# Windowed attention with a mixture of adapters: instruction order from a list scheduler, contiguous score columns, and q and k on 128 partitions

## The chip, the cores and the metric

The kernel runs on one core of one Trainium2 chip. The metric is the device time of one execution in microseconds (us). Executions of one kernel differ by one or two per cent, and the clock that TensorE is granted differs between them too (1.00 is full speed). "Slow" here means over 1.5% above the fastest run of the same kernel in the same group of runs. A profile gives the span from the first to the last instruction; the time of a run is some 1.8 to 2.1 us longer than its span.

Engine names: PE is TensorE's matmuls and PEld its weight loads, DVE is VectorE, ACT is ScalarE, POOL is GpSimd, SP is SyncE, whose queue issues most of the DMA transfers. L396 is line 396 of the kernel that is profiled, so line numbers change from kernel to kernel.

## The reference

```python
# q, k, v: (B=8, H=8, S=576, D=64) float32
scores = (1/sqrt(D)) * q @ k.T
mask   = abs(i - j) <= 32                      # sliding window
attn   = softmax(where(mask, scores, -1e9))
x      = (attn @ v) as (B*S=4608, H*D=512)
# mixture of adapters: E=8 experts of rank r=16, the best two per row
logits = x @ w_gate                            # (4608, 8)
w      = softmax over the two largest logits
out    = x + sum over the two of  w_e * (x @ A[e]) @ B[e]
```

## The kernel before

The work falls into 32 units, one for each pair of heads of each batch (8 batches of 4 units). For a unit, TensorE transposes q and k (`tp`), and the results are copied to SBUF (`qT` and half of `kT` by VectorE, the other half of `kT` by ScalarE). Then come score tiles (`ps`: two mask matmuls and eight score matmuls each), exp on ScalarE (`PT`), the product with v (`po`, "PV" below) and the normalisation on VectorE (`rc`, a RECIPROCAL, then `xb`). After four units the batch's adapters follow: transposes `tx`, logits and low-rank products `pz`, a chain of about ten small VectorE operations (the gate), `zs`, its transpose `tz`, the product `pd`, a ScalarE copy `obt` and the stores. PSUM, the memory that TensorE writes its results to, holds three tiles of 1024 float32 columns (`ps`, `po`, `pz` and `pd` share them; "two-bank tiles" is the prediction's name for them) and two of 1024 float16 columns (the transposes).

The parts that the change and the argument touch (cuts are marked):

```python
ob_pool = tc.alloc_tile_pool(name="ob", bufs=3)
pw = tc.alloc_tile_pool(name="pw", bufs=3, space=bass.MemoryType.PSUM)
pt = tc.alloc_tile_pool(name="pt", bufs=2, space=bass.MemoryType.PSUM)
# ... q and k as loaded and as cast by GpSimd: 96 partitions x 3 groups
raw[b, w] = load_pool.tile([96, 3, 2, NP, 2 * D], F32, ...)
qk[b, w] = cast_pool.tile([96, 3, 2, NP, 2, D], F16, ...)
# ... scores: the two rows of a pair are interleaved in the output columns
        nc.tensor.matmul(
            out=ps[:, i].rearrange("p (k j) -> p j k", j=2),   # stride 2
            lhsT=kTs[u % NQ][:, a, :],
            rhs=qTs[u % NQ][:, :, 32 * a:32 * a + 64], ...)
# ... gate, second part: small VectorE operations on SBUF tensors
    nc.vector.tensor_tensor(out=is2, in0=is2, in1=bcast(dm, 2, E), op=ALU.mult)
    nc.vector.tensor_tensor(out=gate, in0=is1, in1=is2, op=ALU.add)
    nc.vector.tensor_tensor(out=gate, in0=gate, in1=bcast(s, 2, E), op=ALU.mult)
# ... the fixed program order, one unit per turn
for u in range(NU):
    # loads of batch b+2 on nc.sync, casts of batch b+1 on nc.gpsimd
    transposes(u + 2, 0); transposes(u + 2, 1)
    # score(...) for the tiles of unit u+1
    # a piece of the adapters of batch b-1 (moe_out / moe_zl / moe_zT)
    pv(u)
    # another piece of them (moe_xT / moe_gate / moe_out)
```

The softmax here doesn't subtract the row's maximum and nothing guards it: scores larger than these inputs give would overflow.

Of the kernel before, what the change touches and what calls it, by code (L numbers as in the profile page):

```python
# [9 lines left out]
F16 = mybir.dt.float16  # L10
# [14 lines left out]



@with_exitstack
def kernel(
# [18 lines left out]
    NB = 9  # L48
# [25 lines left out]
    def raw_tiles(b):  # L74
        for w in range(2):
            raw[b, w] = load_pool.tile([96, 3, 2, NP, 2 * D], F32, tag=f"r{w}",
                                       name=f"r{w}")
            qk[b, w] = cast_pool.tile([96, 3, 2, NP, 2, D], F16, tag=f"c{w}",
                                      name=f"c{w}")
        raw[b, 2] = load_pool.tile([128, NP * NB, D], F32, tag="r2", name="r2")  # L80

    def load_qk(b, w, eng, n0=0, n1=NP):
        src = (q, k)[w][b]
        if n1 - n0 == NP:
            src = src.rearrange("h (g p j) d -> g p h (j d)", g=3, j=2)
            for g in range(3):
                eng.dma_start(out=raw[b, w][:, g].rearrange("p e n c -> p (e n) c"),
                              in_=src[g])
        else:
            src = src.rearrange("(e n) (g p j) d -> e g p n (j d)", e=2, g=3, j=2)  # L90
            for g in range(3):
                for e in range(2):
                    eng.dma_start(out=raw[b, w][:, g, e, n0:n1], in_=src[e, g][:, n0:n1])

    def load_v(b, eng, n0=0, n1=NP):
        src = v[b].rearrange("(e n) (a p j) d -> e j p (n a) d", e=2, p=32, j=2)
        for e in range(2):
            for j in range(2):
                p0 = 64 * e + 32 * j
                eng.dma_start(out=raw[b, 2][p0:p0 + 32, NB * n0:NB * n1],  # L100
                              in_=src[e, j][:, NB * n0:NB * n1])

    def cast_qk(b, w, eng, n0=0, n1=NP):
        for g in range(3):
            eng.tensor_copy(  # L105
                out=qk[b, w][:, g, :, n0:n1].rearrange("p j n e d -> p e n j d"),
                in_=raw[b, w][:, g, :, n0:n1].rearrange("p e n (j d) -> p e n j d", j=2))

# [13 lines left out]
    raw_tiles(0)  # L122
    for n0 in (0, 2):
        load_qk(0, 0, nc.sync, n0, n0 + 2)
        load_qk(0, 1, nc.scalar, n0, n0 + 2)
        load_v(0, nc.sync, n0, n0 + 2)

    ident = const.tile([128, 128], F16)
    make_identity(nc, ident)


    mask = const.tile([128, 4, 128], F16)
    nc.gpsimd.memset(mask, 0.0)
    for i in range(4):
        jk = i % 2
        blk = mask[32 * i:32 * i + 32]
        nc.gpsimd.affine_select(out=blk, in_=blk, compare_op=ALU.is_ge, fill=NEG,
                                base=-jk, channel_multiplier=-2,
                                pattern=[[0, 4], [1, 128]])
        nc.gpsimd.affine_select(out=blk, in_=blk, compare_op=ALU.is_ge, fill=NEG,  # L140
                                base=64 + jk, channel_multiplier=2,
                                pattern=[[0, 4], [-1, 128]])
# [10 lines left out]

    init_qkT(0)
    init_qkT(1)
    nc.vector.memset(PTs[0], 0.0)
    init_vbd(0)
    nc.vector.memset(PTs[1], 0.0)
# [17 lines left out]
    def transposes(u, which):  # L176
        b, n = divmod(u, NP)
        src = qk[b, which].rearrange("p g j n e d -> p g j n (e d)")
        tp = pt.tile([128, 1024], F16, tag="t", name="tp")
        for g in range(3):  # L180
            for j in range(2):
                if which == 0:
                    o = tp[:, 288 * j + 96 * g:288 * j + 96 * g + 96]
                else:
                    o = tp[:, 192 * g:192 * g + 192].rearrange(
                        "p (a j k) -> p a j k", a=3, j=2)[:, :, j]
                nc.tensor.matmul(  # L187
                    out=o, lhsT=src[:, g, j, n],
                    rhs=ident[0:96, 0:96], is_transpose=True, start=True, stop=True)
        if which == 0:  # L190
            nc.vector.tensor_copy(
                out=qTs[u % NQ][:, :, 16:304],
                in_=tp[:, 0:S].rearrange("p (j s) -> p j s", j=2))
        else:
            kt = tp[:, 0:S].rearrange("p (a k) -> p a k", k=64)
            nc.vector.tensor_copy(out=kTs[u % NQ][0:64, :, 0:64], in_=kt[0:64])  # L196
            nc.scalar.copy(out=kTs[u % NQ][64:128, :, 64:128], in_=kt[64:128])  # L197

    def score(t):
        ps = pw.tile([128, TB, 128], F32, tag="w", name="ps")  # L200
        for i in range(0, TB, 4):
            nc.tensor.matmul(out=ps[:, i:i + 4], lhsT=ident, rhs=mask,  # L202
                             start=True, stop=False)
        for i in range(TB):
            u, a = divmod(TB * t + i, NB)
            nc.tensor.matmul(  # L206
                out=ps[:, i].rearrange("p (k j) -> p j k", j=2),
                lhsT=kTs[u % NQ][:, a, :],
                rhs=qTs[u % NQ][:, :, 32 * a:32 * a + 64],
                start=False, stop=(i % 4 == 3))  # L210
        nc.scalar.activation(out=PTs[t % NPT][:, :, 64:192], in_=ps,  # L211
                             func=AF.Exp, scale=1.0 / float(D) ** 0.5)

    xs = {}

    def pv(u):
        b, n = divmod(u, NP)
        if n == 0:
            xs[b] = x_pool.tile([128, NG, DD], F16, tag="x", name="xb")
        po = pw.tile([128, 1024], F32, tag="w", name="po")  # L220
        for g in range(NG):
# [9 lines left out]
        pog = po[:, 0:GS * NG].rearrange("p (g c) -> p g c", c=GS)[:, :, 0:2 * VD]  # L231
# [6 lines left out]


    st = {}  # L240

    def moe_xT(b, g):
        if g == 0:
            st[b, "xT"] = moe_pool.tile([128, NG, 4, 128], F16, tag="xT", name="xT")
        tp = pt.tile([128, 1024], F16, tag="t", name="tx")
        for c in range(4):
            nc.tensor.matmul(out=tp[:, 128 * c:128 * c + 128],  # L247
                             lhsT=xs[b][:, g, 128 * c:128 * c + 128],
                             rhs=ident, is_transpose=True, start=True, stop=True)
        nc.vector.tensor_copy(  # L250
            out=st[b, "xT"][:, g].rearrange("p c k -> p (c k)"), in_=tp[:, 0:512])
# [11 lines left out]
    def moe_gate(b, part):  # L263
# [10 lines left out]
        if part == 0:  # L274
# [5 lines left out]
            nc.vector.tensor_tensor(out=dm, in0=m2, in1=m1, op=ALU.subtract)  # L280
            nc.scalar.activation(out=dm, in_=dm, func=AF.Exp)
            nc.vector.tensor_tensor(out=is2, in0=lm, in1=bcast(m2, 2, E), op=ALU.is_ge)
            return
        nc.vector.tensor_scalar(out=s, in0=dm, scalar1=1.0, scalar2=None, op0=ALU.add)
        nc.vector.reciprocal(out=s, in_=s)
        nc.vector.tensor_tensor(out=is2, in0=is2, in1=bcast(dm, 2, E), op=ALU.mult)
        nc.vector.tensor_tensor(out=gate, in0=is1, in1=is2, op=ALU.add)
        nc.vector.tensor_tensor(out=gate, in0=gate, in1=bcast(s, 2, E), op=ALU.mult)
        zs = moe_pool.tile([128, NG, E, R], F16, tag="zs", name="zs")
        nc.vector.tensor_tensor(  # L290
            out=zs, in0=pzg[:, :, 0:ER].rearrange("p g (e r) -> p g e r", r=R),
            in1=bcast(gate, 3, R), op=ALU.mult)
# [138 lines left out]
```

## Time and profile before

Median of the three first runs: 227.79 us (226.77 to 229.61). The profiled execution has a span of 225.8 us.

| | before |
|---|---|
| span | 225.8 us |
| busy: TensorE / VectorE / ScalarE / GpSimd | 67 / 50 / 37 / 42% |
| first normalisation, last normalisation | 26.38, 207.69 us |
| mean distance of normalisations | (207.69 − 26.38) / 31 = 5.85 us |
| from the last one to the end | 18.1 us |
| DMA | 38.27 MB, mean 169 GB/s |

The normalisations (VectorE's RECIPROCAL `rc`, one for each unit) are a good clock of progress: the start, the pace and the tail of the kernel can be read from their times.

The page of the kernel before, its first parts and the chain that ended last:

```profile
span 225.8 us, 4064 instructions
PE 152.1 (67%) x1600; PEld 115.3 (51%) x1600; DVE 112.3 (50%) x292; ACT 84.2 (37%) x109; POOL 95.8 (42%) x101
...
PEclk9995896999979999999999966999999988999996
...
PE 25%; DVE 23%; ACT 8%; issue 3%; ACTq 0%
```

No engine is full. The chain alternates between TensorE (25%) and VectorE (23%); in the waits below each waits for the other, VectorE for PV above all (84.0 us). The PEclk row is the granted clock in tenths, for 40 slices of the span.

The waits of the kernel before: who waited for whom, us in total, times, longest us.

```profile
DVE rc L234 <- PE po L226: 84.0, 30, 4.2
ACT kT_93 L197 <- DVE kT_93 L196: 28.6, 8, 3.9
PE tp L187 <- POOL c_99 L105: 15.1, 6, 9.0
```

Each normalisation waits nearly 3 us for its PV; ScalarE's half of the k copies waits for VectorE's half, which stands behind other VectorE work in program order, and the scores wait for that.

The timeline of the kernel before around one score tile (start, us, engine, line, operation):

```profile
153.11 0.97 PEld L206 LDWEIGHTS <-kT_93 128*128 128x128 f16 x8
153.32 1.04 PE L206 MATMUL ps<-qT_89,kT_93 128*128 128x128 f16 x8
...
157.76 1.04 PE L206 MATMUL ps<-qT_86,kT_90 128*128 128x128 f16 x8
158.59 0.64 PE L202 MATMUL ps<-mask,ident 128*128 128x512 f16 x2
```

By their weight loads, eight score matmuls take 0.97 us, 121 ns each, and twelve PV matmuls of about the same size 0.73 us, about 60 ns each.

The windows of the kernel before, in a stretch in which q and k are loaded (the columns are the busy times of the engines; the last three are granted clock, DMA share and GB/s; the DMA share, which can exceed 1, is not used here):

```profile
36.00:40.00 4.00, 3.57 (x37) 2.87 (x36) 1.76 (x4) 1.14 (x3) 3.34 (x3) 0.77 1.23 252
40.00:44.00 4.00, 3.04 (x44) 2.52 (x42) 1.76 (x4) 1.96 (x3) 3.94 (x5) 1.00 1.24 253
```

In these two windows the loads run at 252 and 253 GB/s.

### The profile page before, as it was taken

To read this page: it belongs to the slowest core of one execution; us is meant where nothing else is said; L and a number is where in the kernel's file an instruction comes from. 1 tells how busy PE (TensorE), PEld (TensorE's weight loads), DVE (VectorE), ACT (ScalarE), POOL (GpSimd) and SP (SyncE) were. 2 spreads that over 40 slices of the span, in tenths; PEclk is the share of its full clock that TensorE was granted. 3 is DMA by queue.
4 is the path that set the end of the run, shared out by engine and by line. 5 is a ranking of instruction groups with operands and counts; after the bars stand their busy time and mean duration, and the time that the engine had idled before them with its cause. 6 is when DMAs were issued, how large, how long until landed. Compare 5 with 4: busy or idle time off the path is not lost.

```text
span 225.8 us, 4064 instructions
## 1 busy us (share of the span) xinstructions
PE 152.1 (67%) x1600; PEld 115.3 (51%) x1600; DVE 112.3 (50%) x292; ACT 84.2 (37%) x109; POOL 95.8 (42%) x101
## 2 busy tenths in 40 slices
PE   0354858788387864797686678797768759784740
PEld 0132747666265743575554566575547546562420
DVE  7677333448735354438426552449343553636520
ACT  0240433423263243624561414524662326241351
POOL 8979836948843734437263526055340000000000
PEclk9995896999979999999999966999999988999996
DMA  6999999999969986599939990699622102201325
GB/s 179 237 214 203 235 204 248 251 215 243 227 113 250 252 225 115 147 257 244 193 101 261 234 232 17 188 252 257 142 99 78 35 3 75 99 3 35 131 79 209
DMA packets 85458, 38.27 MB, mean 169 GB/s; under 512 B 43840, under 2 KB 80832, under 8 KB 85440
## 3 DMA queue, kind: packets, MB, share of 16 engines
q1 hardware_dynamic: 78112, 36.58, 70.0%
q0 software_dynamic: 4832, 0.27, 3.6%
q10 hardware_dynamic: 2496, 1.18, 1.9%
q8 instruction: 12, 0.20, 0.4%
q14 instruction: 6, 0.05, 0.1%
HBM read 28.85 MB, written 9.44 MB: 170 GB/s over the span
## 4 chain that ended last, share of the span: by engine, by line
PE 25%; DVE 23%; ACT 8%; issue 3%; ACTq 0%
PE po L226 7%; DVE xb L235 6%; PE ps L206 4%; PE pd L310 3%; PE pz L258 3%; DVE xT L250 3%; PE pd L312 3%; PE tx L247 2%; DVE zs L290 2%; DVE rc L234 2%; PE tp L187 2%; ACT kT_93 L197 1%; ACT kT_92 L197 1%; ACT kT_91 L197 1%; ACT obt L315 1%
## 5 line engine op out<-in xcount | busy, mean ns | idle before, releaser
L234 DVE RECIPROCAL rc<-po 128x10 f32<-128x10 f32 x32 | 7.0, 220 | 84.0 <-PE po L226 84.0
L235 DVE TENSOR_TENSOR xb<-po,rc 128x640 f16<-128x640 f32 x32 | 26.4, 824 | 1.1
L315 ACT COPY obt<-pd 128x1024 f32<-128x1024 f32 (+1 forms) x24 | 20.5, 865 | 12.8 <-PE pd L312 8.1
L202 PE MATMUL ps<-mask,ident 128*128 128x512 f16 x72 | 23.2, 405 | 3.0 <-DVE xb L235 1.9
L206 PE MATMUL ps<-qT_87,kT_91 128*128 128x128 f16 x72 | 12.2, 342 | 13.6 <-ACT kT_91 L197 13.6
L247 PE MATMUL tx<-ident,xb 128*128 128x128 f16 x160 | 13.8, 218 | 9.2 <-DVE xT L250 9.2
L310 PE MATMUL pd<-B_sb,zT 128*128 128x512 f16 x40 | 16.4, 409 | 3.0 <-ACT zT L302 3.0
L206 PEld LDWEIGHTS <-kT_91 128*128 128x128 f16 x72 | 7.9, 134 | 18.1 <-ACT kT_91 L197 15.9
L250 DVE COPY xT<-tx 128x512 f16<-128x512 f16 x40 | 15.4, 419 | 2.7 <-PE tx L247 0.4
L247 PEld LDWEIGHTS <-xb 128*128 128x128 f16 x160 | 10.2, 97 | 12.1 <-issue 11.1
L206 PE MATMUL ps<-qT_86,kT_90 128*128 128x128 f16 x72 | 12.1, 341 | 5.6 <-ACT kT_90 L197 5.6
L312 PE MATMUL pd<-xb,ident 128*128 128x512 f16 x40 | 15.7, 394 | 0.0
L197 ACT COPY kT_93<-tp 64x576 f16<-64x576 f16 x8 | 5.1, 633 | 28.6 <-DVE kT_93 L196 28.6
L206 PEld LDWEIGHTS <-kT_90 128*128 128x128 f16 x72 | 8.1, 136 | 10.3 <-ACT kT_90 L197 7.7
L187 PE MATMUL tp<-ident,c_99 96*128 96x96 f16 x24 | 3.0, 241 | 15.1 <-POOL c_99 L105 15.1
L206 PE MATMUL ps<-qT_88,kT_92 128*128 128x128 f16 x72 | 10.6, 306 | 3.8 <-ACT kT_92 L197 3.8
L197 ACT COPY kT_91<-tp 64x576 f16<-64x576 f16 x8 | 5.1, 633 | 21.5 <-DVE kT_91 L196 21.4
L206 PE MATMUL ps<-qT_89,kT_93 128*128 128x128 f16 x72 | 10.6, 306 | 2.9 <-ACT kT_93 L197 2.6
L211 ACT ACTIVATE PT_94<-ps 128x1024 f16<-128x1024 f32 x9 | 9.2, 1023 | 6.8 <-PE ps L206 6.8
L211 ACT ACTIVATE PT_95<-ps 128x1024 f16<-128x1024 f32 x9 | 9.2, 1023 | 5.7 <-PE ps L206 5.7
L258 PE MATMUL pz<-WA_sb,xT 128*128 128x136 f16 x160 | 11.1, 224 | 0.0
L211 ACT ACTIVATE PT_96<-ps 128x1024 f16<-128x1024 f32 x9 | 9.2, 1023 | 4.5 <-PE ps L206 4.4
(191 smaller groups left out, 362.9 us busy)
## 6 DMA issues: line engine op xcount, KB each, us to landing
out_dram<-obt SPq DMA_DIRECT2D x24, 256.0 KB, 2.8
out_dram<-obt SPq DMA_DIRECT2D x16, 192.0 KB, 2.2
r_98<-in_q_dram SPq DMA_DIRECT2D x12, 96.0 KB, 3.0
r_100<-in_k_dram ACTq DMA_DIRECT2D x12, 96.0 KB, 3.2
r_102<-in_v_dram SPq DMA_DIRECT2D x8, 144.0 KB, 3.3
r_247<-in_q_dram SPq DMA_DIRECT2D x3, 384.0 KB, 7.3
r_249<-in_k_dram SPq DMA_DIRECT2D x3, 384.0 KB, 10.2
r_251<-in_v_dram SPq DMA_DIRECT2D x4, 288.0 KB, 7.1
```

What stands on the lines that cost most here:

```text
L197: nc.scalar.copy(out=kTs[u % NQ][64:128, :, 64:128], in_=kt[64:128])
L202: nc.tensor.matmul(out=ps[:, i:i + 4], lhsT=ident, rhs=mask, start=True, stop=False)
L206: nc.tensor.matmul(out=ps[:, i].rearrange("p (k j) -> p j k", j=2), lhsT=kTs[u % NQ][:, a, :], rhs=qTs[u % NQ][:, :, 32 * a:32 * a + 64], ...
L211: nc.scalar.activation(out=PTs[t % NPT][:, :, 64:192], in_=ps, func=AF.Exp, scale=1.0 / float(D) ** 0.5)
L226: nc.tensor.matmul(out=po[:, GS * g:GS * g + 2 * VD], lhsT=PTs[t % NPT][:, sl, off:off + 128], rhs=vbd[b % NV][:, n, a, :], start=(i == 0) ...
L235: nc.vector.tensor_tensor(out=xs[b].rearrange("p g (e n d) -> p g e n d", e=2, n=NP)[:, :, :, n], in0=pog[:, :, :, 0:D], in1=bcast(rc, 3, ...
L247: nc.tensor.matmul(out=tp[:, 128 * c:128 * c + 128], lhsT=xs[b][:, g, 128 * c:128 * c + 128], rhs=ident, is_transpose=True, start=True, st ...
L250: nc.vector.tensor_copy(out=st[b, "xT"][:, g].rearrange("p c k -> p (c k)"), in_=tp[:, 0:512])
L258: nc.tensor.matmul(out=pz[:, GS * g:GS * g + ER + E], lhsT=xT[:, g, c, :], rhs=WA_sb[:, c, :], start=(c == 0), stop=(c == 3))
L310: nc.tensor.matmul(out=pd[:, i], lhsT=zT[:, g], rhs=B_sb, start=True, stop=False)
L312: nc.tensor.matmul(out=pd[:, i], lhsT=ident, rhs=xs[b][:, g], start=False, stop=True)
L315: nc.scalar.copy(out=ob[:, 0:n], in_=pd[:, 0:n])
```

## The change

Three things change together. The hand-written order is replaced by a plan: each piece of work is entered with its engine, an estimated duration, a due time and what it depends on; a list scheduler simulates the engines and the PSUM pools and emits the instructions in the order that results. The scores are written with contiguous columns: the rows of a unit are permuted, the mask with them, and two matmuls that had the identity as one operand (`tz` and the residual in `pd`) use a permutation matrix instead. And q and k lie on 128 partitions in two groups plus a remainder of 32, instead of on 96 in three groups. By its intent TensorE gets cheaper scores and fills its waits, and GpSimd needs fewer casts.

```diff
+class Plan:
+    def op(self, eng, dur, due, emit, deps=(), alloc=None): ...
+    def emit(self, tail):            # list scheduling: earliest start, then due time
+        ... (cut)
-            raw[b, w] = load_pool.tile([96, 3, 2, NP, 2 * D], F32, tag=f"r{w}",
+            raw[b, w] = load_pool.tile([128, 2, 2, NP, 2 * D], F32, tag=f"r{w}",
+                raw[b, 3] = load_pool.tile([64, 2, NP, 2 * D], F32, tag="r3", name="r3")
... (cut)
+    c_ident = P.op("POOL", 4.5, -99, init_consts)
+    c_perm = P.op("POOL", 0.4, 20, init_perm, [c_ident])
+    c_w = P.op("POOL", 5.0, 21, load_weights, [c_perm])
... (cut; loads: the plan's durations for issuing and for moving them)
+                cnt = 4 if w == 2 else (3 if f == 1 else 6)
+                iss = P.op(eng, 0.5 * cnt, d + w / 10, fn, ring)
+                xfer = P.op("DMA", (4.6 if w == 2 else 3.4) * f, d + w / 10,
+                            lambda: None, [iss])
... (cut; scores)
-                out=ps[:, i].rearrange("p (k j) -> p j k", j=2),
-                rhs=qTs[u % NQ][:, :, 32 * a:32 * a + 64],
+                out=ps[:, i], lhsT=kTs[u % NQ][:, a, :],
+                rhs=qTs[u % NQ][:, :, 32 * a:32 * a + 64].rearrange(
+                    "p j (h k) -> p h j k", h=2),
... (cut; on the way out)
-                             rhs=ident, is_transpose=True, start=True, stop=True)
+                             rhs=perm, is_transpose=True, start=True, stop=True)
-            nc.tensor.matmul(out=pd[:, i], lhsT=ident, rhs=xs[b][:, g],
+            nc.tensor.matmul(out=pd[:, i], lhsT=perm, rhs=xs[b][:, g],
... (cut; stores, on SyncE's queue as before)
+            o = P.op("ACT", 0.93 if len(gs) == 2 else 0.53, d,
+                     lambda gs=gs, h=h: moe_ob(b, gs, h), [pd] + P_pd.get(len(P_pd) - 3, []))
+            s_ = P.op("SP", 0.45 * len(gs), d + 3, lambda gs=gs, h=h: moe_st(b, gs, h), [o])
... (cut)
-    for u in range(NU):              # the fixed order, removed
+    P.emit({"PE": 0.22, "DMA": 0.0})
```

## The prediction

> **What bounds the kernel now.** No engine is full: the page has TensorE 67%, VectorE 50%, ScalarE 37%, GpSimd 42% of 225.8 us. After 64 us it is a chain of waits through in-order queues. Normalisations (VectorE RECIPROCAL, 32 of them, 26.4 to 207.7 us) come every 5.85 us. In the waits view, VectorE waits 84 us for the PV matmuls; scores wait 26 us for the k copies on ScalarE, which wait behind VectorE's, which stand in program order behind norm, gate and xT copies. The chain alternates TensorE (25% of the span), VectorE (23%), ScalarE (8%). DMA is the next limit: 38.3 MB at about 250 GB/s in full stretches (windows view); loads alone took 15.0 us per batch (q issues at 32.4, 47.5, then 62), and stores (1.18 MB) add about 4 us, my estimate from that rate, against 23.4 us per batch of compute.
>
> **What the change does.**
> 1. Score columns contiguous. In the timeline eight score matmuls of 128 columns take 0.97 us of weight loads (121 ns each), twelve PV matmuls of 130 columns 0.73 us (about 60 ns). [...] I blame the stride-2 output. Estimate: 288 x 61 ns = 17.6 us of TensorE, 0.55 us per unit. About half was on the chain. The permutation matmul replaces the identity one: no cost.
> 2. List order: PE, VectorE and ScalarE queues interleave by readiness, so copies for scores no longer queue behind gate work and TensorE fills its waits. Worth most of the gain. TensorE's work per unit, by gaps in the timeline: transposes 0.7, scores 1.0, PV 0.77, adapters 1.2 (a quarter of 4.8), about 3.7 us; VectorE 3.2, ScalarE 2.6. With three two-bank PSUM tiles, I expect 4.4 to 5.0 us per unit.
> 3. q/k on 128 partitions: casts go from six of 1.04 us to five per batch; packets stay 512 B (q, k) and 256 B (v). [...] no gain in bandwidth.
> 4. Start: GpSimd's mask building ran to 8.15 us, and its weight DMA issues (13.9 to 19.0) blocked the second half's casts (TensorE idle 14.6 to 19.75). Shorter mask, later weights: first PV at about 18 us instead of 25.4.
>
> **Sum.** First norm at 18, then 31 units at 4.75 = 147, then tail 17 (207.7 to the end today, same dependent chain): 182 us. DMA alone: 3 + 8 x 15 + five batches of stores x 4 = 143 for the last v, plus some 22 for its cast, two units and the tail: 165 at the least, so it starts to bind the later batches. The kernel's planned durations understate loads (11.4 us per batch against 15), so some queues will stall in order on late data.
>
> **Shown right by:** score matmuls near 60 ns apart; RECIPROCALs 4.4 to 5.0 us apart; VectorE's wait for PV well under 84 us; GB/s near 240 almost to the last load; TensorE busy time about 130 us; first PV before 20 us; GpSimd waiting more for DMA.
>
> **Wrong if:** misjudged transfers make TensorE's queue stall on transposes of data not landed (waits on GpSimd casts over 20 us in total); stores and loads block each other in SyncE's queue; the three PSUM tiles bind; the clock throttles more; or the score rate isn't from the stride.
>
> Predicted 182 us, 8 in 10 between 171 and 198; faster by over 2% 0.96, within 2% 0.03, slower 0.01.

Passages that rested on figures which no trace or run of this case shows are cut, with the cuts marked. No term of the sum goes with them: 18 + 147 + 17 = 182 us. The 61 ns of step 1 are 121 minus about 60, the weight loads of scores and PV in the trace before; to blame the stride was inference, which the first experiment tests. "No cost" of the permutation matmul holds in the traces: from the start of a residual matmul to the next work it is 0.21 us with the identity (101.66 to 101.87 before) and 0.21 with the permutation (60.53 to 60.74 after).

## The result, and the profile after

The median of the four runs of the rounds is 200.77 us (198.17 to 201.32, one of them slow; a fifth run took 201.06), against 228.70 us for the kernel before in the same rounds. The ratio is 0.8778, with a 95% interval of 0.8664 to 0.8892. All ratios here are the mean time of one kernel's fast runs over the mean of the other's fast runs of the same rounds, so not quite the ratio of the medians that are quoted.

The kernel is faster, as predicted, but 200.77 us lies above the predicted range of 171 to 198. The profiled run (198.17 us, span 196.4) was the fastest of the five.

| | before | predicted | after |
|---|---|---|---|
| time | 227.79 | 182 | 200.77 |
| first normalisation | 26.38 | 18 | 23.45 |
| 31 units, us each | 181.3, 5.85 | 147, 4.75 | 153.2, 4.94 |
| from the last one to the end | 18.1 | 17 | 19.7 |
| TensorE busy | 152.1 | about 130 | 144.3 |

The page of the changed kernel:

```profile
span 196.4 us, 4088 instructions
PE 144.3 (73%) x1600; PEld 103.8 (53%) x1600; DVE 113.8 (58%) x290; ACT 84.9 (43%) x109; POOL 84.1 (43%) x91
...
PEclk9999999999958999999669999999669999999966
...
PE 15%; DVE 8%; ACT 2%; issue 1%; ACTq 1%
```

The chain that can be followed through TensorE and VectorE has shrunk from 48% to 23% of the span. Still no engine is full. The clock row has three dips in mid-kernel, where the windows show 0.50. The kernel before has dips too (0.60 from 136 to 140 us, 0.58 from 184 to 188), and the mean clocks of the two profiles are close (0.939 before, 0.931 after).

The waits of the changed kernel:

```profile
DVE rc L450 <- PE po L437: 15.1, 15, 2.7
ACT kT L368 <- DVE kT L366: 17.2, 20, 3.6
PE tp L352 <- POOL c L189: 12.4, 4, 11.4
ACT obt L553 <- DMA out_dram<-obt: 6.1, 2, 3.2
PE ps L396 <- DVE zs L523: 4.7, 2, 2.4
```

VectorE's wait for PV fell from 84.0 to 15.1 us: the main promise of the list order is kept. Of the 12.4 us that TensorE waits for these casts, 11.4 are the one wait at the start; casts of the remainder of 32 partitions add 4.5 us. The last two lines are new. They look small, but they are the ends of the two threads that the experiments follow.

The first thread, in the timeline of the changed kernel where the clock falls for the second time:

```profile
91.69 0.20 DVE L520 TENSOR_TENSOR gate<-is,is 128x40 f32<-128x40 f32 x1
91.83 4.33 POOL L203 CAST vbd<-r 64x2304 f16<-64x2304 f32 x2 [3.81 <-PE po L437]
91.92 2.06 DVE L521 TENSOR_TENSOR gate<-gate,s 128x40 f32<-128x40 f32 x1
94.02 0.82 DVE L523 TENSOR_TENSOR zs<-pz,gate 128x640 f16<-128x640 f32 x1
94.89 1.01 PE L396 MATMUL ps<-mask,ident 128*128 128x512 f16 x2 [2.30 <-DVE zs L523]
```

A VectorE operation on 40 columns, which takes 0.20 us elsewhere, takes 2.06 us. It starts 0.09 us after GpSimd began two casts of v, 2.17 us each, and ends when the first of them ends. I take it that the cast holds it: of the six lines of the gate with operations that took 0.85 to 2.06 us here at the longest, against 0.16 to 0.20 in the median, five read two SBUF tensors, while `zs`, which reads one input from PSUM, took its usual 0.82 us beside the second cast. How the cast holds it was not shown. Two SBUF inputs are not the only case, though: `s`, which has one input, in SBUF, took 1.03 us at 50.95, beside casts that ran from 49.93 to 51.95, against 0.16 at 91.20. Meanwhile TensorE stood for 2.30 us, and in the windows of the changed kernel its clock then falls to a half:

```profile
92.00:96.00 4.00, 1.70 (x13) 1.00 (x14) 3.93 (x5) 0.00 (x0) 3.94 (x2) 0.79 1.07 300
96.00:100.00 4.00, 2.78 (x17) 1.61 (x15) 1.50 (x4) 2.24 (x3) 0.16 (x1) 0.50 1.05 354
```

The longest gaps of TensorE just before the three falls to half clock were 2.06, 2.30 and 2.42 us (they ended at 50.96, 94.89 and 137.90), and the windows in which the clock fell (52 to 56, 92 to 96, 136 to 140) hold 1.66, 1.70 and 1.83 us of TensorE work. A gap of 2.49 us that ended at 44.96 was followed by full clock. So the length of one gap does not decide here; what does was not shown.

The second thread, in SyncE's DMA queue and on ScalarE in the timeline of the changed kernel:

```profile
57.43 1.01 ACT L553 COPY obt<-pd 128x1024 f32<-128x1024 f32 x1 [1.32 <-PE pd L548]
...
64.71 5.82 SPq L181 DMA_DIRECT2D r<-in_v_dram  x4
70.63 3.42 SPq L167 DMA_DIRECT2D r<-in_q_dram  x3
74.15 3.02 SPq L560 DMA_DIRECT2D out_dram<-obt  x5
...
80.16 2.04 ACT L553 COPY obt<-pd 128x1024 f32<-128x1024 f32 x2 [2.93 <-DMA out_dram<-obt]
```

The first results were in their buffer at 58.4 us and their store was issued at 74.15, because five batches of loads and the q of a sixth stand ahead of it in the same queue. The next batch's copy waits for that store: 2.93 us, by the last line.

### The profile page after: what moved, and what is told of

Read it like the earlier page. It is cut to its first block, busy times and chain, and to the rows that moved or that the text cites. A ratio compares the mean times of both kernels' runs of the same rounds, so it can differ in the third digit from the quotient of the medians.

```text
span 196.4 us, 4088 instructions
## 1 busy us (share of the span) xinstructions
PE 144.3 (73%) x1600; PEld 103.8 (53%) x1600; DVE 113.8 (58%) x290; ACT 84.9 (43%) x109; POOL 84.1 (43%) x91
## 2 busy tenths in 40 slices
DMA packets 85810, 38.28 MB, mean 195 GB/s; under 512 B 44192, under 2 KB 81184, under 8 KB 85792
## 5 line engine op out<-in xcount | busy, mean ns | idle before, releaser
L352 PE MATMUL tp<-ident,c 128*128 128x128 f16 (+1 forms) x384 | 35.9, 215 | 22.0 <-POOL c L189 12.4
L408 ACT ACTIVATE PT<-ps 128x1024 f16<-128x1024 f32 x36 | 36.6, 1025 | 33.5 <-PE ps L401 33.4
L203 POOL CAST vbd<-r 64x2304 f16<-64x2304 f32 (+1 forms) x20 | 34.9, 1747 | 23.4 <-DMA out_dram<-obt 9.3
L189 POOL CAST c<-r 128x1024 f16<-128x1024 f32 (+1 forms) x36 | 31.7, 899 | 28.0 <-issue 14.4
L352 PEld LDWEIGHTS <-c 128*128 128x128 f16 (+1 forms) x384 | 25.3, 100 | 34.0 <-POOL c L189 13.1
L437 PE MATMUL po<-vbd,PT 128*128 128x130 f16 x416 | 30.1, 222 | 4.6 <-ACT obt L553 3.3
L437 PEld LDWEIGHTS <-PT 128*128 128x128 f16 x416 | 25.3, 98 | 7.1 <-ACT obt L553 3.9
L368 ACT COPY kT<-tp 64x576 f16<-64x576 f16 x32 | 20.3, 634 | 19.1 <-DVE kT L366 17.2
L401 PEld LDWEIGHTS <-kT 128*128 128x128 f16 x288 | 20.3, 102 | 10.6 <-issue 1.7
L401 PE MATMUL ps<-qT,kT 128*128 128x128 f16 x288 | 24.3, 228 | 0.3 <-ACT kT L368 0.2
L450 DVE RECIPROCAL rc<-po 128x10 f32<-128x10 f32 x32 | 6.8, 214 | 15.1 <-PE po L437 15.1
```

Source lines behind the costliest of these rows:

```text
L189: eng.tensor_copy(out=qk[b, w][:, g, :, n0:n1].rearrange("p j n e d -> p e n j d"), in_=raw[b, w][:, g, :, n0:n1].rearrange("p e n (j d) - ...
L203: eng.tensor_copy(out=dst[64 * e:64 * e + 64, NB * n0:NB * n1, VD * e:VD * e + D], in_=raw[b, 2][64 * e:64 * e + 64, NB * n0:NB * n1])
L352: nc.tensor.matmul(out=o, lhsT=src[:, g, j, n] if g < 2 else sx[p0:p0 + 32, j, n], rhs=ident[p0:p0 + np_, p0:p0 + np_], is_transpose=True, ...
L401: nc.tensor.matmul(out=ps[:, i], lhsT=kTs[u % NQ][:, a, :], rhs=qTs[u % NQ][:, :, 32 * a:32 * a + 64].rearrange("p j (h k) -> p h j k", h= ...
L408: nc.scalar.activation(out=PTs[t % NPT][:, :, 64:192], in_=holder["t"], func=AF.Exp, scale=1.0 / float(D) ** 0.5)
L437: nc.tensor.matmul(out=po[:, GS * g:GS * g + 2 * VD], lhsT=PTs[t % NPT][:, sl, off:off + 128], rhs=vbd[b % NV][:, n, a, :], start=(i == 0) ...
```

## The experiments

The kernels of one group ran one after the other on one chip, with the same runs of the kernel before between them; another group may have had another chip, so across groups I compare ratios to the kernel before. "Ratio" is always to the kernel before, from fast runs, with its 95% interval. The theories at the outset were: (A) the gain is the list order's and the rest is neutral; (B) faster scores carry a good part, as predicted; and, for the missing 19 us, (C) the late start, (D) the gate held by casts, (E) output buffers freed late, and (F) a lower clock that gives part of any TensorE saving back.

### Group 1: the parts one by one

**Contiguous columns alone.** The kernel before, with the changed score columns.

```diff
-                out=ps[:, i].rearrange("p (k j) -> p j k", j=2),
-                rhs=qTs[u % NQ][:, :, 32 * a:32 * a + 64],
+                out=ps[:, i],
+                rhs=qTs[u % NQ][:, :, 32 * a:32 * a + 64].rearrange(
+                    "p j (h k) -> p h j k", h=2),
+    (mask pattern reordered; perm for ident in tz and pd)
```

> The kernel before with only the contiguous score columns, the reordered mask and the permutation matmul; its program order and 96-partition loads stay. Theory (my prediction, step 1): the stride-2 output halves the score rate, so score matmuls go from about 121 ns apart to about 57 ns, TensorE saves about 17 us in all, about half of it on the chain: ratio to before about 0.96, some 8 to 9 us. Rival: the score rate comes from something else (weights, moving operand): matmuls stay near 120 ns apart, ratio 1.00. Second rival: the rate doubles, but in a chain of waits it is hidden: under 3 us gained.

Measured: 227.43 us, ratio 0.9977 (0.9897 to 1.0056): the same. The timeline of this kernel, to be read against 0.97 and 1.04 us before:

```profile
151.32 0.65 PEld L212 LDWEIGHTS <-kT 128*128 128x128 f16 x8
151.53 0.61 PE L212 MATMUL ps<-qT,kT 128*128 128x128 f16 x8
```

The changed kernel shows the same 0.61 us, and when its next work starts:

```profile
66.04 0.61 PE L401 MATMUL ps<-qT,kT 128*128 128x128 f16 x8
66.49 0.61 PE L473 MATMUL tx<-ident,xb 128*128 128x128 f16 x8
```

The 0.61 us overlap the next work, which starts 0.45 us after the first score matmul; that makes 56 ns for each of the eight, against 104 by the same measure before (0.83 us, from 157.76 to 158.59). So the rate nearly doubled, and I put it down to the stride of the output: the edit makes the reading of q no simpler (four runs of 32 columns instead of two of 64). The prediction had compared 121 ns with PV's 60, both from weight loads; from start to start the saving is 48 ns each, 13.7 us for 288 matmuls and not 17.6. (A later expectation's 64 ns is 121 minus the 57 expected here.) But the time did not move. VectorE still waits 82.8 us for PV: TensorE reached its next wait earlier and stood there.

**q and k on 128 partitions alone.** The kernel before, with the changed tiles.

```diff
-            raw[b, w] = load_pool.tile([96, 3, 2, NP, 2 * D], F32, ...)
+            raw[b, w] = load_pool.tile([128, 2, 2, NP, 2 * D], F32, ...)
+        raw[b, 3] = load_pool.tile([64, 2, NP, 2 * D], F32, tag="r3", name="r3")
+    (loads, casts and transposes for it)
```

> The kernel before with only q and k on 128 partitions (loads, casts and transposes as in the changed kernel), program order and stride-2 columns kept. My prediction said no gain in bandwidth. The trace of the changed kernel says otherwise: about 310 to 340 GB/s in full stretches against 250 and 13.4 us between q issues of neighbouring batches against 15.0. If the 128 partitions alone do that, the first three intervals between q issues here are near 13.5 us and q/k stretches near 320 GB/s. If it was the new order or the emptier queue, they stay near 15 us and 250 GB/s. Time either way near before, ratio 0.98 to 1.00, since the kernel before is not bound by loads after 64 us.

Measured: 230.28 us, ratio 1.0086 (0.9969 to 1.0203): no gain in time. But the windows of this kernel show the same stretch of loads faster than the 252 and 253 GB/s before:

```profile
36.00:40.00 4.00, 4.00 (x34) 3.30 (x32) 1.77 (x4) 1.04 (x2) 2.98 (x4) 0.59 0.94 273
40.00:44.00 4.00, 3.71 (x40) 2.64 (x38) 1.77 (x4) 1.84 (x3) 3.70 (x4) 1.00 1.15 336
```

The prediction's "no gain in bandwidth" is wrong for these loads. It looked at packet sizes, which hardly changed (by the pages of the kernel before and the changed one, 43840 and 44192 packets under 512 B, and 36992 in both from there to 2 KB), and not at partitions. The windows mix q, k and v, and v lies as before. From the second whole batch's q issue to the third's it took 12.9 us here, against 15.0 before, a ratio of 0.86; the interval before that one was not shorter (18.6 against 17.6). What in the layout makes the loads faster was not shown: the partitions of a transfer of q or k changed (96 to 128, and a remainder of 32), and its size too (384 KB before; 512 and 128 KB in the changed kernel, which has the same layout).

**Both together, without the list order.** The two edits above in one kernel.

```diff
+    (contiguous columns and 128 partitions, both as above, in the kernel before)
```

> Both of the above together: the changed kernel without its list order. If the parts add, ratio near 0.95, and the list order is worth the rest down to 0.878, about 16 us (my prediction: most of the gain). Rival: the list order is worth little and the two data changes together already give 0.90 or less.

Measured: 229.05 us, ratio 1.0053 (0.9966 to 1.0141): the same. With the order the ratio is 0.8778, so the whole gain needs the list order: theory A. (The list order on 96 partitions was not run, so what the faster loads are worth in the new order is not shown.)

**The list order with the old, strided scores.**

```diff
-                out=ps[:, i], lhsT=kTs[u % NQ][:, a, :],
+                out=ps[:, i].rearrange("p (k j) -> p j k", j=2), lhsT=kTs[u % NQ][:, a, :],
+    (mask and perm as they were)
```

> The changed kernel with the stride-2 score output put back (natural mask order, the permutation matrix is an identity), the list order's planned 0.90 us for a score tile left as it is. If the score rate matters more when TensorE is fuller, this costs 10 us or more over the changed kernel (ratio to before 0.92 or more). If the list order hides it, under 4 us (ratio 0.895 or less).

Measured: 200.61 us, ratio 0.8793 (0.8714 to 0.8873), against 0.8778 for the changed kernel: the faster scores are worth nothing measurable in it either. TensorE's busy time is 157.2 us in this profile against 144.3, so 13 us of TensorE work vanished into waits. (The profile is of a slow run of 203.85 us; its busy time is used only for this coarse comparison.) The clock of its fast runs was 0.938 to 0.956, against 0.903 to 0.931 for the changed kernel. That was the reason to test the clock as a rival, in group 4. Theory B falls.

### Group 2: what holds the changed kernel back

**Weights later.** Theory C: the weights' DMA issues stand ahead of the first cast on GpSimd (5.73 to 10.74 us), and the first normalisation came at 23.45 instead of 18 us.

```diff
-    c_w = P.op("POOL", 5.0, 21, load_weights, [c_perm])
     for b in range(B):
         plan_loads(b)
+        if b == 0:
+            c_w = P.op("POOL", 5.0, 21, load_weights,
+                       [c_perm] + [P_cast[0, w, 2] for w in range(4)])
```

> The changed kernel with GpSimd's six weight DMA issues (5.73 to 10.74 us in its trace) placed after the casts of batch 0. Theory: they hold up the first cast, so the first cast starts near 8.5 us instead of 10.74 and the first norm comes near 21 instead of 23.45; total gain 1 to 3 us (ratio to before near 0.868). Rival: the q data is only there at about 10.5 us, then nothing moves. Against both: the gain is eaten by the loads, which still pace the first batches (norm of unit 8 as late as before, 64.6 us).

Measured: 204.16 us, ratio 0.8942 (0.8854 to 0.903), no gain. The first normalisation came 2.2 us earlier (21.21), but the fourth 0.9 us later (35.25 against 34.33), and one later batch took 30.47 us. The start was partly mis-sized for this reason, but moving the weights bought nothing here; group 3 repeats it where nothing else disturbs.

**Gate temporaries in PSUM.** Theory D. The columns of the `pz` tile beyond the logits are free; four temporaries go there, so that no gate operation reads two SBUF tensors. The arithmetic is unchanged.

```diff
+            st[b, "m2"] = pzg[:, :, ER + E]
+            st[b, "dm"] = pzg[:, :, ER + E + 1]
-            nc.vector.tensor_tensor(out=is2, in0=is2, in1=bcast(dm, 2, E), op=ALU.mult)
-            nc.vector.tensor_tensor(out=gate, in0=is1, in1=is2, op=ALU.add)
-            nc.vector.tensor_tensor(out=gate, in0=gate, in1=bcast(s, 2, E), op=ALU.mult)
+            is2p = pzg[:, :, ER + E + 8:ER + E + 16]
+            gatep = pzg[:, :, ER + E + 16:ER + E + 24]
+            nc.vector.tensor_tensor(out=is2p, in0=is2, in1=bcast(dm, 2, E), op=ALU.mult)
+            nc.vector.tensor_tensor(out=gatep, in0=is1, in1=is2p, op=ALU.add)
+            nc.vector.tensor_tensor(out=gate, in0=gatep, in1=bcast(s, 2, E), op=ALU.mult)
```

> The changed kernel with four of the gate's small temporaries moved into unused columns of the logits' PSUM tile, so that no two-input VectorE instruction of the gate has both inputs in SBUF. Theory: those instructions are held by GpSimd's casts [...] (2.06 us instead of 0.20 in the batch at 92 us), TensorE then [...] runs at half clock for 8 us in three batches. Then: no gate instruction above 0.4 us, the three half-clock stretches (56, 98, 142 us) gone or shorter, mean granted clock up from 0.93, gain 6 to 14 us (ratio to before 0.82 to 0.85). Rival: the stall is TensorE waiting for one of three two-bank PSUM tiles while the gate chain runs at its normal length; then the instructions get short but the half-clock stretches stay and the gain is under 4 us.

Measured: 197.64 us, ratio 0.8647 (0.8538 to 0.8756). That is 1.5% below the changed kernel's ratio, and the intervals overlap. Yet much moved: no gate operation takes over 0.20 us, also beside a cast (lines below), the half-clock stretches near 56, 98 and 142 us are gone, and measured from the fourth normalisation of one batch to that of the next, three batches take 18.1 to 18.4 us, where the changed kernel's lie between 19.93 and 22.58 but for the last. Another takes 29.11 us, and the one after it 22.57, with the clock at a half from about 80 to 88 us. Its timeline, first the gate beside a cast, then the stop:

```profile
95.44 4.33 POOL L203 CAST vbd<-r 64x2304 f16<-64x2304 f32 x2 [5.05 <-PE po L437]
95.62 0.20 DVE L525 TENSOR_TENSOR gate<-pz,s 128x40 f32<-128x40 f32 x1
...
53.28 1.93 ACT L557 COPY obt<-pd 128x1024 f32<-128x1024 f32 x2 [0.47 <-PE pd L552]
...
72.25 3.53 SPq L167 DMA_DIRECT2D r<-in_q_dram  x3
75.89 2.94 SPq L564 DMA_DIRECT2D out_dram<-obt  x5
...
81.40 2.00 ACT L557 COPY obt<-pd 128x1024 f32<-128x1024 f32 x2 [9.80 <-DMA out_dram<-obt]
82.46 1.59 PE L437 MATMUL po<-vbd,PT 128*128 128x130 f16 x13 [8.47 <-ACT obt L557]
```

The results of the first batch were ready at 55.2 us, and their store was issued at 75.89, still behind the loads. The next batch's copies came sooner than before and had to wait 9.80 us for the buffers; ScalarE's queue stood, and TensorE 8.47 us with it. What the repaired gate won, the second hold took back: theory E became the next suspect.

**Casts of v in quarters.** A rival way to shorten the hold: casts of a quarter of the columns (0.67 us each in the run, against 2.14 for whole ones in the changed kernel).

```diff
-        for e in range(2):                      # 64x2304 at a time
+        for m in range(n0, n1):
+            for e in range(2):                  # 64x576 at a time
                 eng.tensor_copy(out=dst[64*e:64*e+64, NB*m:NB*m+NB, ...], in_=...)
```

> The changed kernel with each v cast on GpSimd cut into pieces of 64x576 (about 0.6 us, eight per batch instead of two of 2.17). If the length of one GpSimd instruction sets how long VectorE is held, no gate instruction is above about 1.1 us (the q and k casts' length) and the gain is a part of that of the run with the gate in PSUM, 2 to 8 us. If VectorE is held for as long as GpSimd is busy at all, nothing changes or it gets worse.

Measured: 200.45 us, ratio 0.8702 (0.8581 to 0.8822). The longest gate operation fell from 2.06 to 1.04 us: that one, the one-input `s` at 69.94, stands beside a cast of the q and k remainder of 1.04 us, and beside the short casts of v none takes over 0.70 us. So in these runs the hold follows the length of a cast. The total stayed: there is a gap of 14.8 us between two normalisations at 93.9 to 108.6, at the store.

**Late weights and gate in PSUM together.**

```diff
+    (both edits above, in the changed kernel)
```

> Late weight issues and the gate in PSUM together. If the two causes are separate, gains add: 8 to 16 us below the changed kernel, ratio to before 0.81 to 0.845. If the loads (13.4 us per batch plus about 4 of stores) take over as the limit, the sum is less than the parts, and waits of TensorE for GpSimd casts and of GpSimd for DMA grow.

Measured: 197.87 us, ratio 0.8689 (0.8629 to 0.875), as with the gate alone; one batch took 31.43 us in the same place.

### Group 3: both holds

**Gate in PSUM and six output buffers.** The order of instructions on every engine is identical to the gate kernel's.

```diff
     (gate in PSUM as above)
-    ob_pool = tc.alloc_tile_pool(name="ob", bufs=3)
+    ob_pool = tc.alloc_tile_pool(name="ob", bufs=6)
-                     ..., [pd] + P_pd.get(len(P_pd) - 3, []))
+                     ..., [pd] + P_pd.get(len(P_pd) - 6, []))
```

> The run with the gate in PSUM, and six output buffers instead of three; every engine's order of instructions stays the same. Theory: with the gate stalls gone, TensorE stops 8.5 us at 74 us because the output copy waits 9.8 us for a free output buffer, whose store stands behind five batches of loads in SyncE's queue (first store issued at 75.9 us though its data was ready before 62). Then: no wait of the output copy for a store above 1 us, the batch periods of 29.1 and 22.6 us (norms of units 11 to 15 and 15 to 19) fall to 18 to 19, gain 8 to 14 us over that run, ratio to before 0.80 to 0.83, near the 182 us I predicted. Rival: the loads are the limit there and the stall only moves: less than 4 us gained.

Measured: 183.52 us (182.98 to 184.85), ratio 0.8039 (0.7976 to 0.8102). The missing time is here: 17 us below the changed kernel, and no copy waits for a store any more. Its clock row, and two batches of its windows:

```profile
PEclk9999999699999999999999999999999999979855
...
61.50:79.60 18.10, 16.18 (x204) 12.35 (x202) 12.67 (x36) 9.64 (x14) 12.58 (x10) 1.00 1.07 253
79.60:97.70 18.10, 16.18 (x203) 12.32 (x201) 10.61 (x32) 10.96 (x15) 10.23 (x8) 1.00 1.03 283
```

From the third on, batches take 18.1 to 18.4 us, the last one 17.2, the clock is full from 36 to 160 us, no gate operation takes over 0.20 us, and TensorE is busy 16.18 of 18.10 us, 89%. Now TensorE is the fullest engine (VectorE, the next, has 12.67 us). The pace is 4.42 us per unit (23.99 to 161.07).

**Six output buffers alone.** As above, without the gate edit.

```diff
-    ob_pool = tc.alloc_tile_pool(name="ob", bufs=3)
+    ob_pool = tc.alloc_tile_pool(name="ob", bufs=6)
```

> The changed kernel with six output buffers alone; order unchanged on every engine. In the changed kernel the output copy waits only 6.1 us in two places for stores, behind stalls that the gate makes anyway. Theory of two limits in series: under 3 us gained (ratio 0.865 to 0.88). If the store queue was the only cause all along, the gain is that of both together (ratio 0.83 or less).

Measured: 187.5, 196.52, 195.71 and 197.59 us, at clocks of 0.96, 0.918, 0.918 and 0.909. Only the first counts as fast. The same program has two outcomes, near 187 and near 196; the other three runs are slow only by the rule of this kernel's own best run: their clock is that of the changed kernel's fast runs, and they lie some 4 us below those. What decides between the outcomes I did not show.

**Both, with late weights.**

```diff
+    (gate in PSUM, six buffers, late weights)
```

> Gate in PSUM, six output buffers, and the weight issues after the casts of batch 0. The first norm comes at about 21.3 instead of 24 us. If compute paces the rest, the end comes 2 to 3 us earlier than without the late weights; if loads pace the first three batches, nothing or under 1 us.

Measured: 184.76 us, ratio 0.8082 (0.8016 to 0.8148), against 183.52. The first normalisation came at 21.87 instead of 23.99 us, the eighth at 52.5 instead of 53.0: most of the earlier start is lost by then. My reading is that the first batches run as fast as their loads arrive. Theory C is settled as far as it can be moved: the late start is real, and taking 2.1 us of it away gains nothing.

**Both, with strided scores.**

```diff
-                out=ps[:, i], ...
+                out=ps[:, i].rearrange("p (k j) -> p j k", j=2), ...   (gate in PSUM, six buffers)
```

> Gate in PSUM, six output buffers, and the stride-2 score output put back. With the other stalls gone TensorE should be the fullest engine, so the score rate should at last be worth something: 288 score matmuls x 64 ns = 18 us of TensorE, of which I expect 6 to 14 us in the time (ratio to before 0.84 to 0.88). Rival: the score rate is hidden whatever the rest does (under 3 us).

Measured: 189.74 us, ratio 0.8286 (0.8219 to 0.8354), against 0.8039: some 6 us slower. Once TensorE is that full, the faster scores do count, though with less than half of the 13.7 us that 48 ns each make (the busy times of the two profiles, 151.8 and 140.3 us, differ by 11.5; the strided one is of a slow run).

### Group 4: the clock, and whether it is the queue or the buffers

At this point it was open whether the saving of contiguous columns had been hidden behind waits or given back by a lower clock (theory F), and whether late stores could be cured without more buffers.

**Contiguous columns, with every mask matmul done twice.** This adds useless TensorE work to the first experiment's kernel. The second mask matmul overwrites the first, so the result is the same. The 0.215 us expected for each is half of the 0.43 us from the start of a pair to the next work (40.11 to 40.54 in the changed kernel).

```diff
-        for i in range(0, TB, 4):
-            nc.tensor.matmul(out=ps[:, i:i + 4], lhsT=ident, rhs=mask, start=True, stop=False)
+        for r, i in ((0, 0), (0, 4), (1, 0), (1, 4)):
+            nc.tensor.matmul(out=ps[:, i:i + 4], lhsT=ident, rhs=mask, start=True, stop=(r == 0))
```

> The kernel before with contiguous columns, and each of the 72 mask matmuls run twice (the first result is overwritten): 72 x 0.215 = 15.5 us of useless TensorE work, about what the contiguous columns had saved. If the saving was given back through the clock, this is no slower than the run with the columns alone (ratio to before 0.98 to 1.00) and the granted clock is up from 0.90 to 0.93 or more. If the saving was merely hidden behind waits, the added work is hidden too, ratio 0.99 to 1.01, but the clock does not move. If TensorE's work is on the chain, it is 5 us or more slower than with the columns alone.

Measured: 228.01 us, ratio 0.9977 (0.9877 to 1.0077), the same ratio as without the extra work; TensorE's busy time rose from 145.8 to 155.9 us. The clocks were 0.904 to 0.92, within those of the first experiment (0.889 to 0.923). So TensorE had room for the work: in the old order a saving on it is hidden behind waits. The clock did fall when the columns became contiguous (0.911 to 0.954 before, 0.889 to 0.923 with them, fast runs of the same rounds; 0.964 to 0.975 strided against 0.949 to 0.956 in group 3), but 10 us more work did not bring it back up, as a give-back by the clock would need. Whether the lower clock costs time of its own stays open.

**Casts in quarters and six buffers.** If any shorter hold is enough, this should equal the best kernel.

```diff
+    (casts of v in quarters, six buffers)
```

> The changed kernel with the v casts in pieces of 0.6 us and six output buffers; the gate's temporaries stay in SBUF. If the length of one GpSimd instruction is what counts, no gate instruction is above 1.1 us, half-clock stretches are rare, and the time is near that with the gate in PSUM and six buffers (183.5 us): 184 to 190. If any overlap with GpSimd is enough, it is like six buffers alone: 194 to 198 in most runs.

Measured: 186.22, 197.49, 194.45 and 194.78 us, clocks 0.95, 0.918, 0.926 and 0.926: two outcomes again. Shorter holds do not do reliably what no holds do.

**Stores on ScalarE's DMA queue, three buffers, gate in PSUM.**

```diff
-            nc.sync.dma_start(out=out[r0 + lo:r0 + hi], in_=holder["o"][lo:hi, i])
+            nc.scalar.dma_start(out=out[r0 + lo:r0 + hi], in_=holder["o"][lo:hi, i])
-            s_ = P.op("SP", 0.45 * len(gs), d + 3, ...)
+            s_ = P.op("ACT", 0.05 * len(gs), d, ...)
```

> Gate in PSUM, three output buffers, and the 40 stores issued from ScalarE's DMA queue instead of SyncE's. If the order of SyncE's queue is what held the output buffers, the 9.8 us wait is gone and the time is 182 to 188 us, as with six buffers. If the DMA engines themselves are too busy to take the store earlier, it stays near 197. ScalarE's own issue time could cost a few us.

Measured: 229.34 us, ratio 1.0041 (0.9944 to 1.0139): the whole gain of the change is lost. The waits of SyncE's queue in this kernel:

```profile
SPq L167 <- DMA out_dram<-obt: 56.0, 14, 13.3
SPq L172 <- DMA out_dram<-obt: 24.1, 7, 12.6
```

Now the loads are issued late, after waits that the trace ends with stores. I do not know why the loads' issues depend on the stores here, and whether the chip or the waits that this program sets are the cause is open. As a test of queue against buffers it failed.

**Gate in PSUM, three buffers, and a plan with the measured issue times.** The plan had taken 1.5, 1.5 and 2.0 us to issue a batch's q, k and v; in the trace of the changed kernel, before its first store, they take 3.2 to 3.6, 3.5 to 4.5 and 5.8 to 6.3 us for the batches from 30.16 us on, so that a batch's issues fill SyncE's time: 13.6 us of the 13.9 us from one q issue to the next (30.16 to 44.06). The plan thus thought that SyncE would be free much earlier than it is, and put loads ahead of stores without seeing what that costs.

```diff
-                iss = P.op(eng, 0.5 * cnt, d + w / 10, fn, ring)
-                xfer = P.op("DMA", (4.6 if w == 2 else 3.4) * f, d + w / 10,
+                iss = P.op(eng, (3.4, 4.2, 5.8)[w] * f, d + w / 10, fn, ring)
+                xfer = P.op("DMA", 0.5, d + w / 10,
```

> Gate in PSUM, three output buffers, and the plan told what SyncE's issues take in the trace (q 3.4, k 4.2, v 5.8 us per batch instead of 1.5, 1.5 and 2.0). The list then puts the first stores behind four batches of loads instead of six. If the plan's understated loads are the cause, time falls to 182 to 190 us; since other queues are reordered too, a worse order elsewhere could hide it, then the wait of the output copy for stores still goes below 3 us in total.

Measured: 182.31 us (181.22, 183.15, 181.46; one slow run of 186.06), ratio 0.7982 (0.7897 to 0.8067). The first store in its timeline, to be read against 74.15 in the changed kernel:

```profile
58.12 3.64 SPq L564 DMA_DIRECT2D out_dram<-obt  x5
```

With three buffers as before, stores that are placed right do what three more buffers did, and no copy waits for a store in the waits view. The first store stands behind four batches of loads instead of five and a part. So theory E, as this run shows it, is about when the store is issued; more buffers merely bear a late one. (The edit moves loads as well as stores, since it is the whole plan that comes out differently.) The span is 179.4 us: first normalisation at 22.43, 4.42 us per unit, tail 20.1.

### Group 5: the plan alone, and the tail

**The plan's issue times alone, gate in SBUF.**

```diff
+    (the plan edit above, in the changed kernel)
```

> The changed kernel with only SyncE's issue times in the plan set right (q 3.4, k 4.2, v 5.8 us per batch); gate in SBUF, three output buffers. If the store order was the main cause, this alone gives 182 to 188 us with little spread. If the gate's stalls behind casts count on their own, it is 190 to 198 us in most runs with half-clock stretches in the profile (granted clock 0.91 to 0.93), as with six buffers alone, and gate instructions of 1 to 2 us are still seen.

Measured: 185.36 us fast (clock 0.935); 189.21, 188.7 and 194.75 slow (0.928, 0.924, 0.918). Gate operations are held for up to 2.03 us again and the clock row shows dips to a half. The one fast run is 185.4 us against 181.2 to 183.2 for the same kernel with the gate in PSUM, in another group. One fast run is too little to size the two parts, but it fits with both being needed.

**All of it, six buffers, and the last batch's transposes and logits given an earlier due time.**

```diff
     (gate in PSUM, measured issue times, six buffers)
+        early = 3 if b == B - 1 else 0
-            t = P.op("PE", 0.23, due_u(U, 0.1 + g / 10), ...)
+            t = P.op("PE", 0.23, due_u(U, 0.1 + g / 10 - early), ...)   (same for xT and pz)
```

> Gate in PSUM, plan with SyncE's issue times, six output buffers, and in the last batch the adapter's transposes and logits put before the batch before's output matmuls. From the last norm to the end 1 to 3 us shorter than the 20 us without it; total 179 to 182 us, ratio to before 0.78 to 0.80. If the order in the last batch does not matter, equal to the run with gate and plan (182 us, 0.798).

Measured: 180.63 and 182.3 us fast, 184.61 and 183.59 slow; ratio 0.8091 (0.7993 to 0.8189). In its profile the tail is 18.8 instead of 20.1 us, but the times cannot be told from the kernel of the last group. This kernel, the last of group 4 and the first of group 3 all beat both kernels; the best median is 182.31 us.

## Why the prediction was wrong

The direction and the main mechanism were right, the size was not. Two steps failed. Step 4 and its "first norm at 18" counted on later weights, which the change does not have: 23.45 us. And the pace of step 2, 31 units of 4.75 us, was summed from work and PSUM tiles with no term for two waits, the gate held by casts and the output copies held by late stores: 4.94 us measured, 4.42 with both waits removed. The sum that gave 182 us went wrong as follows; each line is measured minus predicted, and but for rounding the lines add up to 200.8 − 182 = 18.8 us.

| term | predicted | measured | difference |
|---|---|---|---|
| first normalisation | 18 | 23.45 | +5.4 |
| 31 units | 147 (4.75 each) | 153.2 (4.94 each) | +6.2 |
| tail | 17 | 19.7 | +2.7 |
| time outside the span | 0 | 198.17 − 196.4 | +1.8 |
| median run against the profiled run | 0 | 200.77 − 198.17 | +2.6 |

Of the tail's 2.7 us, 1.1 are a slip: from 207.7 to the end the kernel before takes 18.1 us and not 17. The profiled run was the fastest; why the others took some 2.6 us longer no trace shows.

1. **"About half was on the chain" (scores): failed.** The faster rate was shown (104 to 56 ns when the stride went), the saving mis-sized (13.7 us from start to start, not 17.6). The chain's shares were read as if a shorter step shortens the whole; but TensorE's next step waited for something else. The columns are worth nothing measurable in the old order (0.9977, with 1 inside the interval) or in the changed kernel; extra mask work of 10 us was also free. They are worth 6 us after the two holds are gone. TensorE's busy time came to 144.3 us and not to about 130; even without the holds it is 138.6.
2. **List order "worth most of the gain": right, and more than that.** Without it both other parts give 1.0053; with it 0.8778. VectorE's wait for PV fell from 84.0 to 15.1 us as predicted.
3. **"No gain in bandwidth" (128 partitions): failed, with no effect on the time in the old order.** The layout gives 273 and 336 instead of about 250 GB/s in the same two windows. The prediction counted packet sizes only.
4. **"First PV at about 18 us": failed, by 5.4 us.** The prediction expected later weights; the plan issued them before the first cast, so TensorE's first transposes came at 11.44. Late weights bring these to 6.40, but the first normalisation only 2.2 us forward, and that gains nothing; my reading is that the loads pace the first batches. The other 3 us of the miss stay unexplained.
5. **"4.4 to 5.0 us per unit": right as a range, 4.94, but for other reasons than given.** PSUM tiles were named as the limit. The same three tiles allow 4.42 us per unit once the two holds are removed. What the sum left out were those holds: VectorE's gate held by GpSimd's casts, with TensorE's clock at a half afterwards, and output buffers freed late because stores stood behind loads in SyncE's queue.
6. **"Wrong if".** "Stores and loads block each other in SyncE's queue" came true. "The clock throttles more" is not clear: 0.903 to 0.931 in fast runs against 0.939 in the profile before, but 0.911 to 0.961 in that kernel's fast runs of the later groups; and at 0.938 to 0.956, with strided scores, the changed kernel was no faster. "Waits on GpSimd casts over 20 us" did not come true: 12.4 us for q and k and 4.5 for their remainder, 11.4 of it at the start. The plan's understated issue times were even named in the prediction, but only as a danger for late data, not for late stores.

With both holds gone the predicted 182 us is reached (182.31). That is partly luck: the start (22.43) and the tail (20.1) are longer than predicted there too, and the pace (4.42) is shorter.

How the two holds share the 17 us cannot be split cleanly, because each hides the other. By ratio the gate alone gained 1.5%, the buffers alone about 2% in three runs of four, and together they gave 17 us. Where the second hold was already gone, the gate edit gave more: 183.5 against 187.5 to 197.6 us with six buffers, 182.3 against 185.4 to 194.8 with the measured issue times (the second pair across groups). The first store was issued at 74.15, 75.89 and 79.01 us in the changed kernel, with the gate in PSUM, and with six buffers besides: with the old plan it stays behind the loads, so with three buffers compute that arrives earlier only waits longer (9.80 us for the buffers with the gate in PSUM, against 2.93 in the changed kernel). How much of the gate's part is the hold itself and how much the half clock after it is not separated either. It stays open why the kernels with the gate in SBUF have two outcomes, and why stores on the other queue hold up the loads.

## What to carry to other kernels

A list scheduler inside a kernel is only as good as its durations: give it what the trace shows, above all for the queue that issues DMA, where three issues of q took 3.2 to 3.6 us in the trace against the 1.5 us planned, and where a store behind loads holds its buffer (the first one from 58.4 to 74.15 us before it was even issued). Before crediting a faster step, ask what the engine waits for next; here the nearly doubled score rate was worth nothing until two small waits were gone. And look for small VectorE operations that now and then take ten times their usual time (2.06 against 0.20 us): here most of them read two SBUF tensors while GpSimd was casting, and one operand in PSUM ended that (none over 0.20 us).
